# Sharing a PSUM bank between two transposed row blocks, and spreading ten weight loads

## The chip, the cores and the metric

The kernel runs on one core of a Trainium2 chip. The metric is the device time of one execution in microseconds. Five engines matter here: PE (matrix multiplies and transposes), DVE (vector work), ACT (scalar engine, here almost only exponentials), POOL (small vector work and some transfers) and SP, whose queue issues most transfers.

## The reference

Two layers, each an attention block and an MLP, with the same weights in both layers. The input has 2048 rows of 512 in bf16.

```python
x = A_x
x = x + _A_ref(_layernorm(x), A_wqkv, A_wo)   # 32 heads of 16, softmax over 2048 keys
x = x + _B_ref(_layernorm(x), B_w1, B_w2)     # 512 -> 1792, relu, -> 512
x = x + _A_ref(_layernorm(x), A_wqkv, A_wo)
x = x + _B_ref(_layernorm(x), B_w1, B_w2)
return x
```

The layer norm has no scale or shift. For every head 2048 x 2048 exponentials are needed, and that, in two layers, is most of the work outside PE.

## The kernel before

**Tiling.** Rows come in 16 blocks of 128, held as x_t in SBUF, and in chunks of four blocks (512 rows). In the second layer the last two chunks are halved, so that it has six chunks: two of four blocks and four of two. Everything that contracts over the model width needs the normalised rows transposed: ln_transpose transposes one block xnbuf[i] of 128 x 512 on PE in four pieces of 128 x 128 (L535) into a PSUM bank, and a DVE copy (L576) brings the result, 128 x 512 bf16, into xnT, where four such blocks lie side by side for each of the four pieces of the width. ln_groups makes these steps for the n blocks of a chunk.

**Attention.** The main loop goes slot by slot. A slot computes up to three blocks of scores (128 keys x 512 queries; with half chunks, two of 256 for each block) into one of two PSUM tiles ps_s of three banks (L1356). ACT takes the exponential of two or three of them at once (L1365). In some slots the third block goes to DVE instead, which computes the exponential with integer and multiply steps: a first step for each block (L1051), and then a chain over a pair of blocks (L1092, L1103, L1092, L1107, with L1104 in some). PE multiplies the results with the values into ps_o (L944). When a head's segment ends, DVE copies ps_o to u (L858), a transfer c<-u on the SP queue gathers the softmax sums (L863), DVE takes their reciprocal (L885), u<-c brings it back (L886), and the quotient is formed (L874).

**Filler.** All other matrix work (norm transposes, q, k and v, output projection o, the two halves h and z of the MLP) is cut in groups of pieces which PE runs between the scores of the slots. Their matmuls are at L445. In the main loop these groups all use the one bank ps_f, and each ends in one copy out by DVE.

**What sets the order.** The order of instructions on each engine is written by Python at build time: a planner keeps modelled times for PE (now_pe) and DVE (now_dve), a list of what is made and when, and lists of groups (urgent, work) and DVE tasks. A group starts when what it depends on is made (start_group); fill_pe starts no group while an earlier one still waits for its copy (evac), and work is rationed by owed, which grows by a pace in each slot. A piece costs so many units of 216 ns: one transposed block 1.3. The copy of 512 is booked with 342 ns. Between slots run_dve chooses DVE's next instructions, and a pair of blocks is given to DVE when the modelled backlog allows it; in the first layer, after the first pairs, only when the values of all 16 blocks are made. The planner allows the transfer c<-u 3600 ns (C_LAG). If something is needed that is not made, run_until makes it at once. The engines then run their lists in order, whatever the real times.

**Weights of the MLP.** w1 passes through four buffers w1buf of 128 columns each; when an h group is issued, its after() issues the loads that refill the buffers it used (L681). The last half chunk's MLP stands at the end, written out by hand (L1417 and after). For it, w1_last names 14 homes: four are the w1buf, ten are the halves of the tiles kt01 and kt2, free by then. rest_of_chunk issues those ten loads (L766) on the SP queue when the attention of the fourth of the second layer's six chunks ends. A wait of a transfer is made by the queue that issues it, and the queue keeps its order.

Of the kernel before, what the change touches and what calls it, by code (L numbers as in the profile page):

```python
# [12 lines left out]
BF16 = mybir.dt.bfloat16  # L13
# [12 lines left out]
def kernel(  # L26
# [10 lines left out]
    nc = tc.nc  # L37
    P = 128
# [3 lines left out]
    S, D = x_flat.shape  # L42
# [7 lines left out]
    NDC = D // P  # L50
# [50 lines left out]
    def sb(shape, dt, name):  # L101
        return persist.tile(shape, dt, name=name)
# [33 lines left out]
    xnT = [sb([P, NDC, QS], BF16, f"xnT{j}") for j in range(NQS)]  # L136
# [72 lines left out]
    def bank():  # L209
        if ending[0]:  # L210
            bank_no[0] += 1
            return (ps_f[:], ps_s[0][:, 0, :], ps_s[1][:, 0, :])[bank_no[0] % 3]
        if not wide[0]:
            return ps_f[:]
        n = bank_no[0] % 7
        bank_no[0] += 1
        in_bank[0] = (2, 0) if n == 6 else (n // W, n % W)
        if n == 6:
            return ps_f[:]
        return ps_s[n // W][:, n % W, :]  # L220
# [26 lines left out]
    def mark(key, engine="dve", lag=0.0):  # L247
        made[key] = (engine, (now_pe if engine == "pe" else now_dve)[0] + lag)
# [43 lines left out]
    def group(pieces, makes, deps):  # L292
        g = {"pieces": pieces, "makes": makes, "deps": deps}
        maker.update({k: g for k in makes})
        return g

    def put_evac(cost, fn):
        evac.append((cost, now_pe[0] + PE_TO_DVE, fn))
# [85 lines left out]
    def finish_group():  # L384
        while cur:
            do_piece()
        while evac:
            do_evac()
# [24 lines left out]
    def run_all():  # L413
        while True:
            finish_group()
            g = next(
                (g for q in (urgent, work) for g in q if at(g["deps"], "pe") is not None), None
            )
            if g is not None:
                start_group(g)  # L420
            elif dve_q:
                do_task(next(t for t in dve_q if at(t["deps"], "dve") is not None))
            else:
                break
        assert not (urgent or work)
# [104 lines left out]
        )  # L530

    def ln_transpose(tag, i, b=None, at_bank=None):
        pt = (bank() if b is None else b).bitcast(BF16)
        for c in range(NDC):
            ins = nc.tensor.transpose(  # L535
                pt[:, c * P : (c + 1) * P], xnbuf[i][:, c * P : (c + 1) * P], ident[:]
            )
            if wide[0]:
                uses(ins, in_bank[0] if b is None else at_bank)
        mark(("xT", tag, i), "pe")  # L540
        return pt[:, 0 : NDC * P].rearrange("p (c f) -> p c f", c=NDC)
# [24 lines left out]

    def ln_groups(tag, dst, at_column, n, war):
        groups = []
        for i in range(n):

            def piece(i=i):
                pt = ln_transpose(tag, i)

                def fin():
                    a = at_column + i * P
                    nc.vector.tensor_copy(out=dst[:, :, a : a + P], in_=pt)  # L576
                    mark(("xnT", tag, i))

                put_evac(342, fin)

            groups.append(
                group([(1.3, piece)], [("xT", tag, i), ("xnT", tag, i)], [("xn", tag, i)] + war)
            )
        return groups

    def each(n, *key):
        return [key + (i,) for i in range(n)]
# [89 lines left out]
    def load_w1(n):  # L677

        if n < len(chunks) * NF - NF + NW1:
            ft = n % NF  # L680
            nc.sync.dma_start(  # L681
                out=w1buf[n % NW1][:],
                in_=B_w1[:, ft * P : (ft + 1) * P].rearrange("(c p) f -> p c f", p=P),
            )
            mark(("w1", n), "pe", 4000.0)

    def h_group(l, j, ft, war):
        n = (l * NQS + j) * NF + ft
        xj, a, w = columns(l, j)

        number = QS // w
        fts = range(ft, ft + number)
        made_here = [("h", l, j, f) for f in fts]

        def fin(b):
            out = htp[ft // 2][:, ft % 2 : ft % 2 + number, a : a + w]
            sums = b.rearrange("p (f q) -> p f q", f=number)
            if ending[0]:
                nc.scalar.activation(out=out, in_=sums, func=ACTF.Relu)
            else:  # L700
                nc.vector.tensor_scalar(  # L701
                    out=out, in0=sums, scalar1=0.0, scalar2=None, op0=ALU.max
                )
            for key in made_here:
                mark(key)

        def after():
            for f in range(number):
                load_w1(n + f + NW1)

        return mm_group(
            [
                (w1buf[(n + f) % NW1][:, c, :], xnT[xj][:, c, a : a + w])
                for f in range(number) for c in range(NDC)
            ],
            fin, made_here,
            each(w // P, "xnT", ("ln2", l, j)) + war + [("w1", n + f) for f in range(number)],
            after=after, wide_by=w, sums=number,
        )

# [33 lines left out]
    def rest_of_chunk(l, j):  # L754

        if (l, j) == (1, LAST - 2):
            for ft in range(NF):
                home = (
                    w1buf[((l * NQS + LAST) * NF + ft) % NW1] if ft < NW1
                    else (kt01 + kt2)[(ft - NW1) // 2][:, ft % 2, :].rearrange(  # L760
                        "p (c f) -> p c f", c=NDC
                    )
                )
                w1_last.append(home)
                if ft >= NW1:
                    nc.sync.dma_start(  # L766
                        out=home,
                        in_=B_w1[:, ft * P : (ft + 1) * P].rearrange("(c p) f -> p c f", p=P),
                    )
        b = before(l, j)  # L770
        xj, a, w = columns(l, j)
        n = w // P
        war_h = each(chunks[b][1], "z", *b) if b else []
        work[0:0] = [o_group(l, j, i) for i in range(n)] + ln_groups(
            ("ln2", l, j), xnT[xj], a, n, []
        )
        gs = [h_group(l, j, ft, war_h) for ft in range(0, NF, QS // w)]
        gs += [z_group(l, j, i) for i in range((l, j) == (1, LAST - 1), n)]
        if l == 0:
            gs += ln_groups(("ln1", 1, j), xnT[j], 0, TPC, [])  # L780
            gs.append(k_group(1, 0, j))
            gs += [v_group(1, kb) for kb in range(j * TPC, (j + 1) * TPC)]
            gs += [k_group(1, T, j) for T in range(1, 4)]
        return gs
# [342 lines left out]
    tag = ("ln1", 0, 0)  # L1127
    idle_matmuls(24)
    for e in range(2):
        nc.vector.tensor_reduce(  # L1130
            out=mask[e],
            in_=ident[:].rearrange("p (g e d) -> p e g d", g=4, e=2)[:, e],
# [3 lines left out]
            out=qmask[:, e : e + 1], in0=mask[e], scalar1=SCALE * LOG2E * UNIT, scalar2=None,  # L1136
# [8 lines left out]
    for i in range(TPC):  # L1145
        pt = ln_transpose(tag, i)
# [15 lines left out]
    b = plain(k_mms(0, 0))  # L1162
# [6 lines left out]
    b = plain(v_mms(0))  # L1169
# [3 lines left out]
    for j in range(1, NQS):  # L1173
        tag = ("ln1", 0, j)
# [52 lines left out]
    while units:  # L1227
# [6 lines left out]
        for (sg, kb, g), *_ in banked:  # L1234
            if sg["n"] not in seen:
                seen.add(sg["n"])
                n = sg["n"] + 1
# [11 lines left out]
        half = None  # L1249
        if len(banked) == W and pair_at in (None, no):  # L1250
            mine = banked[-1][0][0]
            if pair_at == no:
                half, take = 1, pairs[-1]["sg"]
            elif (not pairs or pair_no[0] + 1 - pairs[0]["n"] < NP) and ((mine['l'] or ("v", 0, 15) in made or not pairs and ("k", 0, 0, 1) in made) and (not mine['l'] or ('k', 1, 0, NQS - 1) in made or pace < PAIR_PACE)):
# [7 lines left out]
                if now_dve[0] + waiting < now_pe[0] + BACKLOG:  # L1262
# [3 lines left out]
                    for n, sg in enumerate(segs[first : here + FAR]):  # L1266
                        till = sum(x is sg or segs.index(x) < segs.index(sg) for x in ahead)
                        if (
# [4 lines left out]
                            half, take = 0, sg  # L1273
# [74 lines left out]
        b = ps_s[no % 2][:].rearrange("p w q -> p (w q)")  # L1348
# [14 lines left out]
        while len(pend) == NE:  # L1363
            force_v()
        ex = nc.scalar.activation(  # L1365
            out=eb[:, 0 : place[m]], in_=b[:, 0 : place[m]], func=ACTF.Exp,
# [27 lines left out]
        run_dve(0.0, musts)  # L1394
    ending[0] = True
    run_all()
    ending[0], wide[0] = False, True
    users.clear()
    l, j = 1, LAST
    tag = ("ln2", l, j)  # L1400
    tt, n_rows = chunks[l, j]
    rows = range(n_rows)
    _, at_column, width = columns(l, j)
    last = slot[0] % 2
    banks = [(1 - last, w) for w in range(W)] + [(2, 0)]
    more = [(last, w) for w in range(W)] + [(3, 0)]
# [4 lines left out]
    def at_bank(b):  # L1411
        n, w = b
        return ps_s[n][:, w, :] if n < 2 else (ps_f, ps_o)[n - 2][:]
# [38 lines left out]

    half_part(0, range(NF))
    for i in rows:
        pt = ln_transpose(tag, i, at_bank(more[i]), more[i])
        copy = nc.vector.tensor_copy if i % 2 else nc.scalar.copy
        uses(copy(out=xnT[NQS - 1][:, :, part(i)], in_=pt), more[i], "xnT")
    for i in rows:
        add(banks[i], ident[:], x_t[tt + i][:], True, False, "x")
    for ft in range(NF + 1):  # L1460
        if ft < NF:
            b = more[ft % 4]
# [5 lines left out]
            if ft % 2:  # L1468
                out = nc.scalar.activation(out=ht[ft][:, at_column : at_column + width], in_=at_bank(b)[:, 0:width], func=ACTF.Relu)
            else:  # L1470
                out = nc.vector.tensor_scalar(
                    out=ht[ft][:, at_column : at_column + width], in0=at_bank(b)[:, 0:width],
                    scalar1=0.0, scalar2=None, op0=ALU.max,
                )
# [7 lines left out]
    for i in rows:  # L1482
# [3 lines left out]
            out=out_flat[(tt + i) * P : (tt + i + 1) * P, :], in_=x_t[tt + i][:]  # L1486
# [31 lines left out]
```

The softmax here doesn't subtract the row's maximum and nothing guards it: scores larger than these inputs give would overflow.

## Time and profile before

The time is 1597.29 us, the median of 3 runs (1595.71 to 1597.43). The profiled execution has a span of 1593.3 us.

| | busy us | share |
|---|---|---|
| ACT | 1553.2 | 97% |
| DVE | 1490.0 | 94% |
| PE | 1437.3 | 90% |
| POOL | 98.4 | 6% |

| rows that the change touches | count | mean ns |
|---|---|---|
| transpose L535, 128 x 128 into ps_f | 232 | 221 |
| copy L576, 128 x 512 bf16 out of ps_f | 58 | 418 |
| load L681, 128 KB, SP queue | 130 | |
| load L766, 128 KB, SP queue | 10 | |

In a group's row the columns are: line, engine, operation, what is written <- what is read, shapes, count | busy us, mean ns of one | idle time of the engine just before, and what ended it. In a timeline row they are: start in us, duration in us, engine, line, operation; a bracket at the end is idle time before it and what ended that. An engine's busy time is the union of its instructions, which can overlap a little, so that the distance from start to start is shorter than the duration of one.

### The profile page before, as it was taken

Reading aid. Unit: us, or ns where it says so; the run is one execution under the profiler, and the core shown is the slowest. Engines: PE = TensorE matmul, PEld = TensorE weight load, DVE = VectorE, ACT = ScalarE, POOL = GpSimd, SP = SyncE. Lnnn points to the kernel's source line nnn. Section 1 sums busy time; section 2 is a strip of 40 time slices with the busy share of each in tenths; the row PEclk is TensorE's granted clock in tenths of the full one; section 3 lists DMA queues with packets and bytes.
Section 4 is the critical chain, followed back from the end, with each engine's and each line's share of the span. In section 5 each row is a group of like instructions: output and inputs, shape, how many; then the busy total and the mean of one; then the engine's idle time right before and its main releaser. Section 6 shows DMA issues by size and latency. Waiting matters only on the chain.

```text
span 1593.3 us, 45167 instructions
## 1 busy us (share of the span) xinstructions
PE 1437.3 (90%) x19793; PEld 539.0 (34%) x19793; DVE 1490.0 (94%) x2899; ACT 1553.2 (97%) x1383; POOL 98.4 (6%) x240
## 2 busy tenths in 40 slices
PE   8888888998999989899888999888999899899897
PEld 3322222222233222233222223222334444445454
DVE  6669999999999999999899999899999999899994
ACT  7999999999999999999999999999999999899994
POOL 2000001001010010100000000001000110010100
PEclk9999999999999999999999999999999999999999
DMA  5001100210012000120000100000211111413020
GB/s 166 1 2 23 20 11 10 46 29 12 5 22 45 19 15 5 29 46 11 14 2 11 31 8 1 2 4 9 55 24 20 36 36 23 93 20 65 14 61 16
DMA packets 115829, 42.42 MB, mean 27 GB/s; under 512 B 104784, under 2 KB 112720, under 8 KB 115632
## 3 DMA queue, kind: packets, MB, share of 16 engines
q1 hardware_dynamic: 101696, 26.21, 7.3%
q0 software_dynamic: 12592, 12.02, 4.2%
q8 instruction: 154, 2.52, 0.6%
q10 hardware_dynamic: 1344, 1.31, 0.2%
q14 instruction: 43, 0.35, 0.1%
HBM read 24.38 MB, written 2.10 MB: 17 GB/s over the span
## 4 chain that ended last, share of the span: by engine, by line
ACT 72%; PE 14%; DVE 11%; issue 2%; SPq 1%; DMA 0%; POOL 0%; ACTq 0%; DVEq 0%
ACT e L1365 72%; PE ps_s L1356 5%; PE ps_f L445 4%; PE ps_o L944 4%; DVE lin L1051 3%; DVE cube L1103 1%; DVE step L1092 1%; DVE cube L1107 1%; PE ps_s L1417 1%; DVE q L643 1%; DVE ht L701 1%; SPq L766 1%; DVE stats L479 0%; DVE u L858 0%; DVE x L727 0%
## 5 line engine op out<-in xcount | busy, mean ns | idle before, releaser
L1365 ACT ACTIVATE e<-ps_s 128x1536 bf16<-128x1536 f32 (+1 forms) x1366 | 1544.6, 1366 | 9.4 <-PE ps_s L1356 8.5
L1356 PE MATMUL ps_s<-q,ktp 32*128 32x512 bf16 (+1 forms) x6121 | 604.6, 340 | 106.2 <-ACT e L1365 96.3
L944 PE MATMUL ps_o<-e,vaug 128*32 128x512 bf16 (+1 forms) x4256 | 496.3, 345 | 12.4 <-DVE u L858 5.4
L1051 DVE TENSOR_SCALAR lin<-ps_s 128x512 int16<-128x512 f32 x684 | 465.5, 685 | 24.1 <-PE ps_s L1356 17.2
L1356 PEld LDWEIGHTS <-ktp 32*128 32x128 bf16 x6121 | 196.3, 91 | 552.2 <-issue 418.0
L944 PEld LDWEIGHTS <-vaug 128*32 128x32 bf16 x6036 | 171.9, 94 | 298.7 <-issue 281.7
L1092 DVE TENSOR_SCALAR step<-lin 128x1024 int16<-128x1024 int16 x684 | 268.8, 419 | 0.6
L1103 DVE TENSOR_TENSOR cube<-step 128x1024 f16<-128x1024 bf16 x342 | 231.8, 681 | 0.6
L1107 DVE TENSOR_TENSOR cube<-cube,lin 128x1024 bf16<-128x1024 f16 x342 | 232.3, 680 | 0.0
L944 PE MATMUL ps_o<-step,vaug 128*32 128x512 bf16 (+1 forms) x864 | 156.0, 339 | 3.2 <-DVE step L1092 3.2
L445 PE MATMUL ps_f<-xnT,w 128*32 128x512 bf16 (+1 forms) x2016 | 151.0, 347 | 6.1 <-DVE ht L701 2.9
L944 PE MATMUL ps_o<-cube,vthird 128*32 128x512 bf16 (+1 forms) x812 | 148.9, 338 | 0.5 <-DVE cube L1107 0.5
L445 PE MATMUL ps_f<-w,ht 128*32 128x512 bf16 x1624 | 146.7, 381 | 1.1 <-DVE q L643 0.8
L944 PE MATMUL ps_o<-lin,vaug 128*32 128x512 bf16 (+1 forms) x864 | 121.7, 338 | 4.8 <-DVE u L858 1.8
L888 POOL DMA_DIRECT2D r<-u x59 | 43.7, 740 | 1176.8 <-DVE lin L1051 383.2
L445 PE MATMUL ps_f<-xnT,wqkv 128*32 128x512 bf16 (+1 forms) x1312 | 106.6, 360 | 5.4 <-DVE ktp L593 0.9
L445 PE MATMUL ps_f<-wo,ot 128*32 128x512 bf16 x960 | 86.3, 381 | 1.1 <-DVE ktp L593 0.8
L701 DVE TENSOR_SCALAR ht<-ps_f 128x512 bf16<-128x512 f32 x105 | 72.0, 686 | 3.3 <-PE ps_f L445 2.1
L445 PEld LDWEIGHTS <-w 128*32 128x32 bf16 x2016 | 60.0, 97 | 37.3 <-issue 21.7
L643 DVE TENSOR_TENSOR q<-ps_f,masks 128x1024 bf16<-128x1024 f32 (+1 forms) x51 | 53.6, 1051 | 12.4 <-PE ps_f L445 7.6
L445 PEld LDWEIGHTS <-ht 128*32 128x32 bf16 x1624 | 45.3, 96 | 28.3 <-issue 12.2
L944 PEld LDWEIGHTS <-vthird 128*32 128x32 bf16 x812 | 44.5, 95 | 30.6 <-issue 27.1
(103 smaller groups left out, 637.7 us busy)
## 6 DMA issues: line engine op xcount, KB each, us to landing
w<-in_B_w_dram SPq DMA_DIRECT2D x130, 128.0 KB
r<-u POOLq DMA_DIRECT2D x32, 256.0 KB, 7.3
r<-u POOLq DMA_DIRECT2D x27, 128.0 KB, 5.0
out_dram<-x SPq DMA_DIRECT2D x16, 128.0 KB
x<-in_A_x_dram SPq DMA_DIRECT2D x14, 128.0 KB
w<-in_B_w_dram SPq DMA_DIRECT2D x1, 1792.0 KB
ktp<-in_B_w_dram SPq DMA_DIRECT2D x10, 128.0 KB
wqkv<-in_A_wqkv_dram ACTq DMA_DIRECT2D x2, 512.0 KB
```

Of the source, the lines that this page charges most:

```text
L445: nc.tensor.matmul(out[cols], lhsT[:, cols], rhs, start=i % k == 0, stop=i % k == k - 1, tile_position=(0, 32 * g), skip_group_check=True,)
L643: return nc.vector.tensor_mul(out=qbuf[n % 2][:, :, 0:w], in0=b.rearrange("p (e q) -> p e q", e=1).to_broadcast((P, 2, w)), in1=qmask.rear ...
L701: nc.vector.tensor_scalar(out=out, in0=sums, scalar1=0.0, scalar2=None, op0=ALU.max)
L766: nc.sync.dma_start(out=home, in_=B_w1[:, ft * P : (ft + 1) * P].rearrange("(c p) f -> p c f", p=P),)
L888: nc.gpsimd.dma_start(out=r[:, 0:width], in_=bass.AP(tensor=sums.tensor, offset=sums.offset, ap=[list(sums.ap[0]), [0, 32], [1, width]],),)
L944: nc.tensor.matmul(ps_o[32 * g : 32 * g + 32, 0 : sg["w"]], values[:, 4 * sg["T"] + g, 2 * e : 2 * e + 32], rhs, start=g not in sg["begun" ...
L1051: first = nc.vector.tensor_scalar(out=lin[which][:, half * QS : (half + 1) * QS], in0=src, scalar1=EXP_BIAS, scalar2=0.0, op0=ALU.add, op1 ...
L1092: nc.vector.tensor_scalar(out=stair, in0=line, scalar1=keep, scalar2=put, op0=ALU.bitwise_and, op1=ALU.bitwise_or,)
L1103: (609, lambda: nc.vector.tensor_mul(out=power, in0=mantissa, in1=mantissa)),
L1107: (609, lambda: nc.vector.tensor_mul(out=power.bitcast(BF16), in0=power, in1=line.bitcast(BF16))),
L1356: nc.tensor.matmul(b[:, a : a + sg["w"]], kt[32 * g : 32 * g + 32, kc : kc + P], qbuf[sg["n"] % 2][32 * g : 32 * g + 32, sg["e"], 0 : sg[" ...
L1365: ex = nc.scalar.activation(out=eb[:, 0 : place[m]], in_=b[:, 0 : place[m]], func=ACTF.Exp, scale=1.0 / (LOG2E * UNIT),)
```

## The change

Two edits. First, in ln_groups two row blocks share a group: each is transposed into its half of one bank (512 bf16 of the 1024 that fit), and one copy of 128 x 1024, booked with 609 ns, brings both into xnT. This halves the number of copies, of bank turns and of groups. A group now depends on both blocks. The transposes of the first and of the last chunk, which stand outside the main loop, still go one by one. Second, the ten loads for the last MLP are put in a list when they become due, and each later h group issues one, after its own loads, so that they don't fill the SP queue all at once.

```diff
-        for i in range(n):
-
-            def piece(i=i):
-                pt = ln_transpose(tag, i)
+        for i in range(0, n, 2):
+            hold = {}
+
+            def piece(k):
+                if not k % 2:
+                    hold["b"] = bank()
+                half = hold["b"].bitcast(BF16)[:, k % 2 * D : (k % 2 + 1) * D]
+                ln_transpose(tag, k, half)
+                if not k % 2:
+                    return
+                pt = hold["b"].bitcast(BF16).rearrange("p (i c f) -> p c i f", i=2, c=NDC)
 
                 def fin():
-                    a = at_column + i * P
-                    nc.vector.tensor_copy(out=dst[:, :, a : a + P], in_=pt)
-                    mark(("xnT", tag, i))
-
-                put_evac(342, fin)
+                    a = at_column + (k - 1) * P
+                    nc.vector.tensor_copy(
+                        out=dst[:, :, a : a + 2 * P].rearrange("p c (i f) -> p c i f", i=2), in_=pt
+                    )
+                    for of in (k - 1, k):
+                        mark(("xnT", tag, of))
+
+                put_evac(609, fin)
 
             groups.append(
-                group([(1.3, piece)], [("xT", tag, i), ("xnT", tag, i)], [("xn", tag, i)] + war)
+                group(
+                    [(1.3, lambda k=k, piece=piece: piece(k)) for k in (i, i + 1)],
+                    [("xT", tag, k) for k in (i, i + 1)] + [("xnT", tag, k) for k in (i, i + 1)],
+                    [("xn", tag, k) for k in (i, i + 1)] + war,
+                )
             )
...
+    w1_to_load = deque()
...
         def after():
             for f in range(number):
                 load_w1(n + f + NW1)
+            if w1_to_load:
+                home, of = w1_to_load.popleft()
+                nc.sync.dma_start(
+                    out=home,
+                    in_=B_w1[:, of * P : (of + 1) * P].rearrange("(c p) f -> p c f", p=P),
+                )
...
                 if ft >= NW1:
-                    nc.sync.dma_start(
-                        out=home,
-                        in_=B_w1[:, ft * P : (ft + 1) * P].rearrange("(c p) f -> p c f", p=P),
-                    )
+                    w1_to_load.append((home, ft))
```

More of the change, by code (lines that the diff above doesn't have):

```diff
@@ L532, in ln_transpose @@
     def ln_transpose(tag, i, b=None, at_bank=None):
-        pt = (bank() if b is None else b).bitcast(BF16)
+        pt = bank().bitcast(BF16) if b is None else b
         for c in range(NDC):
@@ L1396 @@
     run_all()
+    assert not w1_to_load
     ending[0], wide[0] = False, True
@@ L1454 @@
     for i in rows:
-        pt = ln_transpose(tag, i, at_bank(more[i]), more[i])
+        pt = ln_transpose(tag, i, at_bank(more[i]).bitcast(BF16), more[i])
         copy = nc.vector.tensor_copy if i % 2 else nc.scalar.copy
```

## The prediction

> **What bounds the kernel now.** I read the page first, then the groups with shapes kept apart, then the windows, then the timelines of the one window that stood out.
>
> ```profile
> PE 1437.3 (90%) x19793; PEld 539.0 (34%) x19793; DVE 1490.0 (94%) x2899; ACT 1553.2 (97%) x1383; POOL 98.4 (6%) x240
> ACT 72%; PE 14%; DVE 11%; issue 2%; SPq 1%; DMA 0%; POOL 0%; ACTq 0%; DVEq 0%
> ```
>
> ACT sets the end: it is idle for only 1593.3 - 1553.2 = 40.1 us. The windows say where: 11.5 us before 20 us (the prologue), 21.3 us after 1550 us (the last MLP by hand), and of the 7.2 us between them 4.92 us lie in one window, 1360 to 1400. All other seams together leave 2.3 us. So a change can gain in three ways: fewer exponentials on ACT, a shorter prologue or tail, or that one gap. The page also lists SPq L766, the burst of ten weight loads, at 1% of the chain: a queue that should never be on it.
>
> The groups show what ACT's work consists of and how DVE shares it (columns: count | busy us, mean ns of one | idle before):
>
> ```profile
> L1365 ACT ACTIVATE e<-ps_s 128x1536 bf16<-128x1536 f32 x681 | 1024.1, 1576 | 8.2 <-PE ps_s L1356 7.6 <-PE ps_o L944 0.5
> L1365 ACT ACTIVATE e<-ps_s 128x1024 bf16<-128x1024 f32 x684 | 739.3, 1157 | 1.2 <-PE ps_s L1356 0.9
> L576 DVE COPY xnT<-ps_f 128x512 bf16<-128x512 bf16 x58 | 24.2, 418 | 3.1 <-PE ps_f L535 2.8
> L535 PE MATMUL ps_f<-ident,xn 128*128 128x128 bf16 x232 | 22.9, 221 | 2.6 <-DVE xnT L576 0.8 <-DVE xn L526 0.6 <-DVE q L643 0.5
> ```
>
> Half of the slots hand one block of 512 columns to DVE; that makes the exponential 1576 - 1157 = 419 ns shorter, so a pair of blocks on DVE is worth 0.84 us of ACT. Lines L576 and L535 are all that the first edit touches: 58 copies, 232 transposes.
>
> The window 1360 to 1400, in slices (PE, PEld, DVE, ACT, POOL busy, clock, DMA share, GB/s), and DVE there:
>
> ```profile
> 1375.00:1380.00 5.00, 3.88 (x89) 2.21 (x88) 1.83 (x4) 5.00 (x5) 0.00 (x0) 1.00 0.67 140
> 1380.00:1385.00 5.00, 2.67 (x43) 1.66 (x46) 3.98 (x10) 0.79 (x2) 0.00 (x0) 0.57 0.52 114
> 1385.00:1390.00 5.00, 5.00 (x98) 2.80 (x90) 3.85 (x7) 4.29 (x5) 0.00 (x0) 0.75 0.24 52
> ```
> ```profile
> 1372.76 0.41 DVE L858 COPY u<-ps_o 128x256 f32<-128x256 f32 x1
> ...
> 1376.15 0.68 DVE L1107 TENSOR_TENSOR cube<-cube,lin 128x1024 bf16<-128x1024 f16 x1
> 1380.58 0.20 DVE L885 RECIPROCAL c<-c 128x8 f32<-128x8 f32 x1 [3.75 <-DMA c<-u]
> ```
>
> The sync queue and ACT in the same window:
>
> ```profile
> 1369.87 8.57 SPq L766 DMA_DIRECT2D ktp<-in_B_w_dram  x10
> 1378.54 0.56 SPq L863 DMA_DIRECT2D c<-u  x1
> ```
> ```profile
> 1384.60 1.45 ACT L1365 ACTIVATE e<-ps_s 128x1536 bf16<-128x1536 f32 x1 [4.21 <-PE ps_s L1356]
> 1386.76 14.66 ACT L1365 ACTIVATE e<-ps_s 128x1024 bf16<-128x1024 f32 x13 [0.71 <-PE ps_s L1356]
> ```
>
> Read them as one story. DVE has the softmax sums copied at 1372.76 + 0.41 = 1373.17. Their small transfer c<-u could be issued then, but the sync queue is busy with ten loads until 1378.44. It goes out at 1378.54 and takes 2.02 us (chain of waits); DVE waits 3.75 us for it with all its later work behind, PE waits 3.17 us for DVE (its L944 row at 1382.33), and ACT runs dry for 4.21 us and again for 0.71 us, the second while PE's clock is down at 0.57 to 0.75. Nowhere else does DVE wait longer than 3.8 us for c<-u: the waits list gives it 4.0 us in two waits, this one and a trifle.
>
> **What the skill says.** (1) "DMA: Bandwidth & Descriptors", Anatomy of one DMA: a semaphore wait happens on the issuing sequencer before dispatch, and a transfer has a fixed cost of some 2.0 us. So whatever stands ahead of c<-u on the queue delays it; the trace agrees, with the queue busy for 8.57 us and 2.02 us for c<-u. (2) "VectorE: DVE Perf Modes", Why PSUM operands drop a tier and the table of the errata section: a bf16 copy out of PSUM runs at most two per cycle, 120 + FD/2 cycles at 0.96 GHz: 392 ns for 512 and, an estimate from that page, 658 ns for 1024. The trace has 418 ns for 512, so two per cycle it is. (3) "PSUM — Partial Sum Buffer", The four PSUM rules: a bank is 2 KiB per partition; two blocks of 512 bf16 fill it exactly, so the second block fits. No run here shows that yet. (4) "TensorE: Matmul & The Clock Gate", What's actually happening: a mostly idle PE has its clock lowered. The 0.57 after the 3.17 us wait agrees.
>
> **Part 1, the weight loads.** Removed: the burst. Its ten loads go out one after each h group, behind the one or two loads of w1 that the group issues anyway. L701 rows stand at 1374.95, 1381.26 and 1385.79, so h groups are running when the loads become due, and fourteen more (seven for each of two half chunks) follow before the last MLP needs them. Cost: the same ten issues of about 0.51 us (their median), now spread; the sync queue has room, and no compute engine waits on the loads until 1570 us. A c<-u that comes just after a group finds at most one more load ahead. Gain: in the window above c<-u would go out at about 1373.2 and land at 1373.2 + 0.05 + 2.02 = 1375.3, before DVE turns to the reciprocal at 1376.83. DVE's 3.75 us wait goes, and with it ACT's 4.21 + 0.71 = 4.92 us. Even with one slow load of 2.33 us ahead it lands at 1377.6, a wait of 0.8 us. Bounds: 3.0 us (3.75 less 0.8) to 4.9 us; I take 4.9, since on the free queue nothing else fills the time.
>
> **Part 2, the shared bank.** PE: the same 232 transposes, no change. DVE: 58 copies become 29 of 1024. From start to start the neighbours of such rows show 0.33 us for a 418 ns instruction (L1092 at 1371.82, next at 1372.15) and 0.60 us for a 680 ns one (L1107 at 1370.62, next at 1371.22). I put the 1024 copy in the latter class: twice the 267 ns of streaming plus the same 151 ns is 685 ns. So 58 x 0.33 = 19.1 us becomes 29 x 0.60 = 17.4 us, 1.7 us saved; by the full durations, 24.2 - 29 x 0.685 = 4.3 us. The other end, if the new order of the output (two blocks swapped with four) lost the two per cycle, is the fp32-like row L643 of 1024 at 1220 ns: 29 x 1.14 = 33 us, 14 us lost. I take the first: innermost runs stay 128 elements on both sides, as in the 418 ns copy. DVE's saving counts only as exponentials taken from ACT: a pair costs DVE (465.5 + 268.8 + 231.8 + 232.3 + 10.3) / 342 = 3.53 us and frees 0.84 us, so 1.7 us is worth 0.4 us (4.3 us: 1.0 us).
>
> Moved: the filler groups share one bank, ps_f, and the planner starts no group while one waits to be copied out, so a transpose group takes a slot of about 1.1 us for 0.40 us of PE. Copies in the first stage stand at 38.20, 39.25 and 40.59. Six slots fewer before the last v group (113.0 us) would bring the point at which DVE may take pairs freely, about 115 us, up to 6 x 1.1 = 6.6 us forward. Before that DVE takes 11 first steps in 95 us; afterwards 9 in 15 us. 6.6 x (0.60 - 0.12) = 3.2 blocks of 0.42 us is 1.3 us at most; half-used, as the v groups are held by PE's spare time and not by the bank, 0.6 us. Added waits: a group starts only when both its row blocks are normalised, so the first waits one L526 more (0.33 us), and the bank is held until the second is transposed (0.40 us on PE). Both delay only filler, which has slots of slack while ACT is fed; I cost them at nothing.
>
> **Sum.** 4.9 + 0.4 + 0.6 = 5.9 us; I take 0.2 off for a load that may still stand ahead of a c<-u and use 5.7. 1597.3 - 5.7 = 1591.6 us.
>
> **Rivals.**
> *A new stall takes the old one's place (17%).* The order is written by a planner with estimated costs, so from the first shared bank at 37 us on every group lands elsewhere, and DVE has no slack (94%) to hide a late transfer. One such event costs about what this one did: 5.7 - 4.9 leaves 0.8 us, 1596.5 us. Against: of 78 such transfers before, one did this, and it had a burst ahead of it.
> *Slower by the new order (14%).* Two such stalls, or one and five pairs fewer on DVE (5 x 0.84): 1591.6 + 9.8 = about 1601 us. For: 99% of DVE is booked in most windows; the run before leaves only 2.3 us in seams, little to gain and more to lose. Against: the pairs are gated by queued work, which shrinks.
> *The wide copy falls to one per cycle (4%).* 14 us more DVE: as 4 pairs lost, 3.3 us; as stalls, since the planner books 609 ns, the full 14: 1595 to 1606, centre 1600.
> *More comes of it (10%).* The longer DVE saving (1.0), the whole 1.3 us, and fewer blocked slots in the later filler stages, two or three pairs more: 1591.6 - 3.5 = 1588 us.
>
> **Chances and range.** The forecast, within 2.5 us of 1591.6, has 55%. Faster than 1594.1 (0.2%): nearly all of that and the 10%, 0.66. Within 0.2%: the replaced stall, 0.17. Slower: 0.17. The range reaches from 1587.5, just under the best case, to 1600, which takes in one stall and part of the slower cases.
>
> **What will show it.** L766 gone as a burst; no DVE wait on c<-u above 1 us; ACT's gap list between 20 and 1550 us under 4 us in all; PE's clock at 1.00 there. The copy x29 at about 685 ns (1200 would be the third rival). The first steps L1051 at 684 or a few more; 676 or fewer means the planner gave pairs up. The last v copy of layer 0 at 107 to 112 us. The prediction is wrong if ACT waits for scores appear in the seams at 100 to 130, 550 to 600, 700 to 780 or 1140 to 1180 us.

## The result, and the profile after

The changed kernel takes 1592.40 us, the median of six runs (1591.72 to 1594.34), against 1598.02 us for the kernel before in the same session: a ratio of 0.9968 (here and below not the quotient of the two medians), with a 95% interval of 0.9955 to 0.9980, or 5.1 us with an interval of 3 to 7 us. The forecast was 1591.6 us.

First the page of the changed kernel, with the engines' busy time and the shares of the chain:

```profile
PE 1431.9 (90%) x19801; PEld 538.6 (34%) x19801; DVE 1490.7 (94%) x2876; ACT 1552.1 (98%) x1383; POOL 100.1 (6%) x240
ACT 80%; PE 8%; DVE 8%; issue 2%; DMA 1%; POOL 0%; SPq 0%; ACTq 0%; DVEq 0%
```

ACT's busy time fell by only 1.1 us, yet the chain runs through ACT for 80% of the span and no longer for 72%: what went is time in which ACT had nothing to do. The groups say where the 1.1 us comes from (count | busy us, mean ns of one | idle before):

```profile
L1384 ACT ACTIVATE e<-ps_s 128x1536 bf16<-128x1536 f32 x679 | 1021.1, 1576 | 4.5 <-PE ps_s L1375 3.7 <-PE ps_o L963 0.3
L1384 ACT ACTIVATE e<-ps_s 128x1024 bf16<-128x1024 f32 x686 | 740.8, 1156 | 0.6 <-PE ps_s L1375 0.6
L583 DVE COPY xnT<-ps_f 128x1024 bf16<-128x1024 bf16 x29 | 19.8, 682 | 2.8 <-PE ps_f L535 2.7
L535 PE MATMUL ps_f<-ident,xn 128*128 128x128 bf16 x232 | 20.1, 222 | 2.0 <-DVE xnT L583 1.8
```

Two slots more hand a block to DVE (686 for 684): one pair, 0.84 us of the 1.1; most of the rest is one single exponential of 128x512 that took 597 ns and not 850. The wide copy takes 682 ns, near the forecast 685 and far from the 1220 ns of the slow case (L643 of 1024), so it kept the rate of the narrow copy.

Next the sync queue where the burst used to be:

```profile
1368.31 5.15 SPq L695 DMA_DIRECT2D w<-in_B_w_dram  x4
1373.50 0.50 SPq L728 DMA_DIRECT2D ktp<-in_B_w_dram  x1
1374.10 0.57 SPq L882 DMA_DIRECT2D c<-u  x1
1377.51 1.47 SPq L695 DMA_DIRECT2D w<-in_B_w_dram  x2
1379.02 0.50 SPq L728 DMA_DIRECT2D ktp<-in_B_w_dram  x1
```

One of the ten loads stands ahead of c<-u in place of all ten, behind the four of w1, and c<-u goes out at 1374.10, right when the sums are copied (L877 at 1373.66 + 0.41 us). The windows there (PE, PEld, DVE, ACT, POOL busy, clock, DMA share, GB/s), DVE's reciprocal and ACT:

```profile
1375.00:1380.00 5.00, 4.91 (x134) 2.77 (x126) 5.00 (x12) 5.00 (x7) 0.00 (x0) 1.00 0.28 62
1380.00:1385.00 5.00, 4.64 (x124) 2.82 (x112) 4.74 (x12) 5.00 (x6) 0.00 (x0) 1.00 0.60 135
1385.00:1390.00 5.00, 4.36 (x97) 2.22 (x95) 5.00 (x12) 5.00 (x6) 0.00 (x0) 1.00 0.36 79
```
```profile
1379.86 0.19 DVE L904 RECIPROCAL c<-c 128x8 f32<-128x8 f32 x1
```
```profile
1358.80 42.21 ACT L1384 ACTIVATE e<-ps_s 128x1536 bf16<-128x1536 f32 x38
```

No bracket follows the reciprocal, and ACT runs 42 us without one: no wait, no gap, the clock at 1.00. Between 20 and 1550 us ACT is now idle for 1530 - 1527.25 = 2.75 us; before it was 7.2 us. In the four seams that the prediction named as signs of being wrong, ACT's idle time is 0.28 us in all, and was 1.96 us. Of the 4.5 us so gained and the 1.1 us of busy time, 2.2 us are lost again at the end of this profiled run, where PE's clock fell (0.73 and 0.58) while the last values were summed (ACT's wait for PE that follows is 6.2 us, and 4.2 us before):

```profile
1555.00:1560.00 5.00, 4.20 (x67) 2.26 (x61) 3.98 (x9) 4.79 (x4) 0.00 (x0) 0.73 0.00 0
1560.00:1565.00 5.00, 5.00 (x41) 2.41 (x39) 2.19 (x5) 1.03 (x2) 0.00 (x0) 0.58 0.01 3
```

So the spans of the two profiled runs differ by only 3.4 us. Such drops come and go from run to run; a fit over all runs of this study gives about 0.9 us more for each 0.001 of mean granted clock less. Below, "at equal clock" means the time brought to a clock of 0.995 by that fit: before 1597.3, the changed kernel 1593.3 us (within 0.6). This is a rough measure, and it hides a part of the burst's price: the stall itself took the clock to 0.57 and 0.75 in two windows of 5 us, by which the mean over the span falls by some 0.002 (5 x 0.43 + 5 x 0.25 = 3.4 us of 1593). By the fit that is about 2 us, an estimate, which "at equal clock" leaves out of the burst's price. For each kernel the plain median and its ratio to the kernel before on the same chip come first.

### The profile page after: what moved, and what is told of

Read it like the earlier page. It is cut to its first block, busy times and chain, and to the rows that moved or that the text cites. A ratio compares the mean times of both kernels' runs of the same rounds, so it can differ in the third digit from the quotient of the medians.

```text
span 1589.9 us, 45152 instructions
## 1 busy us (share of the span) xinstructions
PE 1431.9 (90%) x19801; PEld 538.6 (34%) x19801; DVE 1490.7 (94%) x2876; ACT 1552.1 (98%) x1383; POOL 100.1 (6%) x240
## 4 chain that ended last, share of the span: by engine, by line
ACT 80%; PE 8%; DVE 8%; issue 2%; DMA 1%; POOL 0%; SPq 0%; ACTq 0%; DVEq 0%
ACT e L1384 80%; PE ps_s L1375 3%; DVE lin L1070 2%; PE ps_f L445 2%; PE ps_o L963 2%; DVE step L1111 1%; PE ps_s L1437 1%; DVE cube L1126 1%; DVE cube L1122 1%; DVE ht L717 1%; DMA r<-u 0%; DMA wqkv<-in_A_wqkv_dram 0%; DVE q L657 0%; DVE ot L893 0%; DVE stats L479 0%
## 5 line engine op out<-in xcount | busy, mean ns | idle before, releaser
L1384 ACT ACTIVATE e<-ps_s 128x1024 bf16<-128x1024 f32 (+1 forms) x1366 | 1543.4, 1365 | 5.1 <-PE ps_s L1375 4.3
L445 PE MATMUL ps_f<-xnT,w 128*32 128x512 bf16 (+1 forms) x2016 | 146.7, 345 | 5.5 <-DVE ht L717 2.8
L963 PE MATMUL ps_o<-step,vaug 128*32 128x512 bf16 (+1 forms) x868 | 151.0, 340 | 0.0
L963 PE MATMUL ps_o<-cube,vthird 128*32 128x512 bf16 (+1 forms) x816 | 144.1, 338 | 0.0
L445 PE MATMUL ps_f<-wo,ot 128*32 128x512 bf16 x960 | 91.7, 381 | 1.0 <-DVE x L681 0.9
```

Of the source, the lines that this page charges most:

```text
L445: nc.tensor.matmul(out[cols], lhsT[:, cols], rhs, start=i % k == 0, stop=i % k == k - 1, tile_position=(0, 32 * g), skip_group_check=True,)
L963: nc.tensor.matmul(ps_o[32 * g : 32 * g + 32, 0 : sg["w"]], values[:, 4 * sg["T"] + g, 2 * e : 2 * e + 32], rhs, start=g not in sg["begun" ...
L1384: ex = nc.scalar.activation(out=eb[:, 0 : place[m]], in_=b[:, 0 : place[m]], func=ACTF.Exp, scale=1.0 / (LOG2E * UNIT),)
```

## The experiments

**The two edits apart.** The planner doesn't book the loads, so the second edit alone leaves PE, DVE and ACT in the order of before, and the first alone gives them that of the changed kernel. In the traces DVE and ACT keep these two orders, instruction for instruction.

```diff
 # e1_loads: before, with the second edit only
+                    w1_to_load.append((home, ft))
 # e2_bank: after, with the burst kept
-                    w1_to_load.append((home, ft))
+                    nc.sync.dma_start(out=home, in_=B_w1[...])
```

> Only the second edit: ten loads spread, transposes and copies as before. The planner does not book loads, so PE, DVE and ACT get the order of before. Theory (queue order): the 3.75 us wait of the reciprocal and ACT's 4.9 us gap go, and nothing else changes: 3.0 to 4.9 us faster than before, about 1593.5 us. Rival (the gain of the change comes from the new order that the shared bank brings): within 1 us of before, about 1597.5 us.

> Only the first edit: shared bank and wide copy, but the ten loads issued at once as before; engines have the order of the changed kernel. Theory: one pair more on DVE and seams as in the changed kernel, 1 us faster than before by itself, but the burst meets whatever c<-u stands near it; in the changed kernel a c<-u stands at 1374, close after the last loads of h groups, so the burst delays it by up to 6 us and a stall of 0 to 5 us remains: 1593 to 1598 us. Rival (the stall was an accident of the old order): no stall in the new order, the same time as the changed kernel, 1592.4 us.

Loads alone: 1592.05 us against 1597.64, ratio 0.9966 (0.9955 to 0.9977). Bank alone: 1594.28 us, ratio 0.9980 (0.9972 to 0.9988). At equal clock 1593.4 and 1594.9, with 1593.3 for both edits together. The loads alone bring all of the gain, so the first theory holds. Their trace has c<-u on the queue as soon as the sums are copied (1373.65 + 0.42 us), no wait at the reciprocal, and no gap of ACT:

```profile
1374.10 0.56 SPq L868 DMA_DIRECT2D c<-u  x1
```
```profile
1338.93 81.77 ACT L1370 ACTIVATE e<-ps_s 128x1536 bf16<-128x1536 f32 x73
```

Between 20 and 1550 us ACT is idle for 2.6 us there, 4.6 us less than before. That the bank alone brings more than half has its reason mostly in the order: the burst still stands ahead of c<-u, which goes out at 1380.03, but in the new order DVE comes to the reciprocal 5.9 us after copying the sums, and not 3.7 us, so less of the delay shows. DVE and ACT with the bank alone:

```profile
1382.05 0.20 DVE L907 RECIPROCAL c<-c 128x8 f32<-128x8 f32 x1 [1.79 <-DMA c<-u]
```
```profile
1384.77 5.54 ACT L1387 ACTIVATE e<-ps_s 128x1024 bf16<-128x1024 f32 x5 [2.93 <-PE ps_s L1378]
```

1.79 us in place of 3.75, and 2.93 in place of 4.92. The gains of the two edits are not to be added: they are two ways of losing less at one place.

**Fewer loads at once.**

```diff
+                if NW1 <= ft < NW1 + 5:
+                    nc.sync.dma_start(out=home, in_=B_w1[...])
+                elif ft >= NW1:
+                    w1_to_load.append((home, ft))
```

> The kernel before with five of the ten loads at once and five one by one. Theory (queue order): in the trace of before the fifth load is out at about 1372.3 us, before the sums are copied at 1373.2, so c<-u goes out at once, and there is no wait: the time of all ten spread, about 1593.5 us. Rival (any burst on the transfer engines delays c<-u, in proportion): half of the wait stays, about 1.9 us, and 1595.5 us.

1594.06 us, ratio 0.9974 (0.9964 to 0.9985); at equal clock 1593.6, the time of ten spread. In its trace the five take the queue for 3.25 us, to 1377.08, the sums are copied at 1377.14, and c<-u goes out at 1377.17. DVE doesn't wait for it, its wait for the way back u<-c is 0.52 us, and ACT has no gap. What counted for c<-u was that the queue was free when it was wanted; the five loads then under way cost almost nothing.

**The burst on another queue.**

```diff
-                    nc.sync.dma_start(
+                    nc.gpsimd.dma_start(
```

> The kernel before with the burst of ten loads kept in one place, but issued on POOL's queue, so that it moves the same bytes at the same time and doesn't stand ahead of c<-u. Theory (order on the SP queue): the wait of the reciprocal is under 1 us and the time is that of spread loads, about 1593.5 us. Rival (the ten loads fill the transfer engines, and c<-u would be late on any queue): the wait stays at 2 to 4 us and the time within 2 us of before.

1596.78 us, ratio 0.9994 (0.9982 to 1.0006), so no gain by the plain times; at equal clock 1596.1, 1.2 us better than before and 2.7 us short of spread loads. Neither theory alone is right. The wait for c<-u is gone, but new ones are there. POOL's queue, DVE, PE and ACT:

```profile
1378.11 7.83 POOL L766 DMA_DIRECT2D ktp<-in_B_w_dram  x10
```
```profile
1382.56 0.19 DVE L885 RECIPROCAL c<-c 128x8 f32<-128x8 f32 x1
1389.06 0.01 DVE L898 LOAD_MASK_SELECT r<-u  x1 [2.56 <-DMA u<-c]
```
```profile
1386.11 0.73 PE L445 MATMUL ps_f<-xnT,w 128*32 128x256 bf16 x20 [1.09 <-DMA w<-in_B_w_dram]
1387.21 3.28 ACT L1365 ACTIVATE e<-ps_s 128x1536 bf16<-128x1536 f32 x3 [1.20 <-PE ps_s L1356]
```

The way back, u<-c, was issued at 1383.77 on a free sync queue and yet DVE had to wait for it until 1389.06. PE waited too, for a w1 load from the sync queue, and ACT's gap of 1.20 us comes right after that wait, ahead of DVE's. So the burst has a second price, which the order of one queue doesn't explain: while the ten loads were being sent, this small transfer took 5.25 us, where c<-u took 2.02 us in the kernel before. That this is the filling of the transfer engines is a reading; no run took it apart.

**The same burst, one place further back, and a planner that knows of the delay.** In the first of these the ten loads go out at once just behind the c<-u; the engines' order is that of before. In the second the burst stays where it was, and the planner allows this one c<-u 9600 ns; from there on it draws a new order, with one pair more for DVE.

```diff
 # e12_behind, after the issue of c<-u
+                while w1_to_load:
+                    home, of = w1_to_load.popleft()
+                    nc.sync.dma_start(out=home, in_=B_w1[...])
 # e8_lag
-                mark(("c", n), lag=C_LAG)
+                mark(("c", n), lag=C_LAG + (6000.0 if late else 0.0))
```

> The kernel before with its burst of ten loads whole, but issued just behind the one c<-u transfer that it stood ahead of; PE, DVE and ACT keep their order of before. If the late c<-u is all that the burst cost: ACT has no gap near 1375 us and the time is that of spread loads, 1592 to 1594 us. If whatever stands behind the burst pays, the loads of w1 for the next h groups too: PE waits 1 to 4 us for a w1 load, and 1594.5 to 1597.5 us. I take the second, 1595.5 us, after the run with the longer allowance, in which PE waited for such a load.

> The kernel before with its burst of ten loads on the SP queue, but the planner is told that the one c<-u transfer behind the burst takes 9600 ns in place of 3600, so that DVE is given other work first and comes to the reciprocal later. The transfer is as late as before. Theory (what costs is DVE standing at a reciprocal that comes too early in its order, with all else queued behind): the 3.75 us wait shrinks to under 1 us and 3 to 4.5 us are gained, about 1594 us. Rival (the late sums themselves hold up what needs them, the output projection and its followers): no gain, about 1597.5 us.

Behind: 1600.23 us, ratio 1.0018 (1.0007 to 1.0029), even slower than before. Longer allowance: 1599.36 us, ratio 1.0008 (1.0000 to 1.0016), no gain. In both the wait for c<-u is gone. With the burst behind it, PE, DVE and ACT show this instead:

```profile
1385.98 1.26 PE L445 MATMUL ps_f<-xnT,w 128*32 128x256 bf16 x20 [5.12 <-DMA w<-in_B_w_dram]
```
```profile
1387.70 0.01 DVE L902 LOAD_MASK_SELECT r<-u  x1 [5.44 <-DMA u<-c]
```
```profile
1387.83 1.45 ACT L1369 ACTIVATE e<-ps_s 128x1536 bf16<-128x1536 f32 x1 [5.86 <-PE ps_s L1360]
```

The w1 loads for the next h group stand behind the ten, start at 1382.79, and PE is kept from its filler, and so from the scores behind it, for 5.12 us. With the longer allowance the chain of waits goes the same way: a w1 load from 1384.56 for 2.41 us, then PE, and ACT is idle for 2.31 us. That is less than the 4.92 us of before, and yet nothing is gained; since the order is new from here on, the first of the two runs is the cleaner one. The theory that only the reciprocal's place in DVE's order costs has fallen: in each of these runs something else behind the burst paid, and taking one transfer out of the way handed the bill to the next.

**What a microsecond of DVE costs that nobody booked.** Each wide copy is made twice.

```diff
+                    nc.vector.tensor_copy(
+                        out=dst[:, :, a : a + 2 * P].rearrange("p c (i f) -> p c i f", i=2), in_=pt
+                    )
```

> The changed kernel with each of the 29 wide copies made twice, which the planner does not know of: 29 x 0.60 = 17.4 us more on DVE, everything else in the same order. It prices an unbooked DVE microsecond, and so what the forecast's third rival (a wide copy at one element per cycle, 14 us more) would have cost. If DVE time comes out in full: 17 us slower than the changed kernel, about 1610 us. If slack in the order swallows it: under 5 us slower, 1592 to 1597 us. I take 7 us, about 1600 us, since DVE is booked at 99% but its work waits in buffers ahead of PE.

1612.55 us, ratio 1.0086 (1.0072 to 1.0100). DVE is busy for 1507.8 - 1490.7 = 17.1 us more, and at equal clock the time grows by 14.7 us. My guess of 7 us was half of it; nearly the full DVE time comes out.

**How far two orders of the same work lie apart.** Only the number that the planner books for the copy is changed. On the chip the work is nearly the same: with the order the planner also moves a pair or two of blocks between ACT and DVE (first steps on DVE: 684 with the loads alone, 686 in e10_book and e6_book; 686 with both edits, 690 in e7_book, 684 in e9_book) and repeats some matmuls more.

```diff
 # with the loads alone: e6_book, e10_book
-                put_evac(342, fin)
+                put_evac(350, fin)   # e10_book: 338
 # the changed kernel: e7_book, e9_book
-                put_evac(609, fin)
+                put_evac(620, fin)   # e9_book: 600
```

> Loads spread, transposes and copies of one block as before, but the copy booked with 350 ns in place of 342: no work is added, only the planner's order changes. Theory (a new order by itself moves the time little as long as no burst lies in it): within 2.5 us of the kernel with the loads alone, 1590.5 to 1595 us. Rival (a new order is a lottery of several us): more than 3 us away from it.

> The changed kernel with the wide copy booked with 620 ns in place of 609: again only the order changes. Together with the run before it shows how far two orders of the same work lie apart, and so whether the shared bank's own share of the gain can be told from zero. Theory: within 2.5 us of the changed kernel, 1590 to 1595 us. Rival: more than 3 us away.

> The changed kernel with the wide copy booked with 600 ns in place of 609: only the planner's order changes, a second draw of an order for the shared bank beside the one with 620 ns (1592.3 us). If orders of this kernel mostly come out alike: 1590 to 1595 us. If the 21 us that 8 ns of booking cost the kernel with the loads alone is the usual scatter: more than 5 us from 1592.4 us. I think the first has 60%.

> Loads spread, transposes and copies as before, the copy booked with 338 ns in place of 342; a second draw beside the one with 350 ns (1613.4 us), which stood 10.7 us at a reciprocal's round trip that its planner had been forced into. If such forced steps are rare: 1591 to 1596 us. If they are usual in this kernel: over 1597 us. I think the first has 55%.

| kernel | booked ns | us | ratio to before | at equal clock |
|---|---|---|---|---|
| loads alone | 342 | 1592.05 | 0.9966 (0.9955 to 0.9977) | 1593.4 |
| e10_book | 338 | 1595.30 | 0.9991 (0.9978 to 1.0004) | 1595.9 |
| e6_book | 350 | 1613.43 | 1.0097 (1.0084 to 1.0110) | 1609.6 |
| both edits | 609 | 1592.40 | 0.9968 (0.9955 to 0.9980) | 1593.3 |
| e7_book | 620 | 1592.30 | 0.9960 (0.9947 to 0.9973) | 1593.6 |
| e9_book | 600 | 1598.83 | 1.0003 (0.9990 to 1.0016) | 1596.6 |

Of the four draws one equals the order that it starts from (0.3 us apart at equal clock), two are 2.5 and 3.3 us slower and one is 16 us slower. That one has a new stall, at another seam. DVE and POOL's queue in e6_book:

```profile
1183.09 0.25 DVE L890 RECIPROCAL c<-c 128x16 f32<-128x16 f32 x1
1194.04 0.75 DVE L879 SCALAR_TENSOR_TENSOR ot<-u,masks,r 128x512 bf16<-128x512 f32 x1 [10.70 <-DMA r<-u]
```
```profile
1186.73 0.69 POOL L893 DMA_DIRECT2D r<-u  x1 [40.64 <-issue]
```

In DVE's order the product follows the reciprocal at once, though two transfers lie between (1.82 and 7.29 us in the chain of waits). That is what run_until does when a segment ends and its buffer u is still in use; that it was called here follows from the order, it was not recorded. DVE stands for 10.70 us, PE for 9.09, ACT for 9.28 and once more for 4.26 us. e9_book has no stall of that kind. In its profiled run ACT is idle for 10.5 us between 20 and 1550 us, and 7.0 us of that lie in five windows of 10 us with a low clock, such as these:

```profile
840.00:850.00 10.00, 8.88 (x60) 1.90 (x59) 8.38 (x16) 9.17 (x9) 3.49 (x9) 0.65 0.01 2
850.00:860.00 10.00, 10.00 (x70) 2.50 (x67) 7.20 (x15) 7.44 (x7) 0.00 (x0) 0.50 0.00 1
```

The clock isn't the whole of it, since at equal clock e9_book is still 3.3 us slower than the changed kernel; one pair fewer on DVE is worth 0.84 us of that, and the rest stays open.

**A try for a faster version: more work on PE against clock drops.**

```diff
-    FLOOR = 0.56
+    FLOOR = 0.60
```

> The changed kernel with PE's least load raised from 0.56 to 0.60 of a slot, so that it repeats more score matmuls and has fewer drops of its granted clock. Over all runs so far a clock lower by 0.001 goes with 0.8 us more. Theory (the drops cost the time): the mean clock rises from 0.9957 to 0.998 or more and the time falls by about 2 us, to 1590.5 us, if the new order is as good. Rival (the repeated matmuls, or the new order, cost more): slower than 1593.5 us.

1597.48 us, ratio 1.0001 (0.9988 to 1.0014). The mean clock was 0.9946, no higher than the changed kernel's 0.9957, with 230 more matmuls. The theory fell: more repeated matmuls in a new order did not keep the clock up, and at equal clock this order is 4.6 us slower. No run beat the changed kernel beyond doubt; the loads alone and e7_book equal it.

## Why the prediction was right

*Part 1, the loads: right in mechanism and size.* The step said 3.0 to 4.9 us, with 4.9 taken. The loads alone measured 0.34% (0.23 to 0.45), 5.4 us by the ratio and 3.9 us at equal clock (which takes the stall's own clock drop out). The steps inside held as well: the engines' order is unchanged, c<-u goes out when the sums are there, DVE's 3.75 us and ACT's 4.92 us are gone. What was incomplete is the list of who pays. The prediction followed only the reciprocal; the burst kept behind c<-u showed that w1 loads and the way back u<-c pay as much (5.12 and 5.44 us of waiting). It made no difference here because the edit spreads the loads and doesn't only move them.

*Part 2, the shared bank: each term near its size, the sum not seen.* The copy: 685 ns forecast, 682 measured. DVE's saving becoming exponentials taken from ACT: one pair more, worth 0.84 us of ACT, against 0.4 + 0.6 us. The last v copy of the first layer: forecast 107 to 112 us, measured 110.86 us (113.02 before), 2.2 us earlier where I had used half of 6.6. But the loads alone are as fast as both edits within 0.8 us at equal clock, so the 1.0 us that I added for this part can't be shown in the time. Orders of nearly the same work lay 0.3 to 16 us apart, so a gain of 1 us can't be read off.

*The unknown costs at nothing*, the later start and the longer hold of the bank: show on PE only: its idle time ahead of the transposes, waiting for the copy before, went from 0.8 to 1.8 us in all (while all of its idle time there fell from 2.6 to 2.0), and no gap of ACT over 0.15 us comes within 2 us after one of these waits. An order drawn anew would hide a small cost of this kind.

*The rivals.* "A new stall takes the old one's place" and "slower by the new order" did not come. I gave them 31% together, and they were nearer than that: of four further orders two were about 3 us and one 16 us slower at equal clock. The size of the second was too small as well: I had put it at 1601 us, and an 8 ns change of a booking, in the kernel with the loads alone, gave 1613 us, which lies outside my range. So the time came out as forecast for the reason given, with a share of luck in the order that the shared bank drew. The third rival, a copy at one element per cycle, would have cost nearly its upper end: 17.1 us of unbooked DVE gave 14.7 us, so 14 us would give about 12, an estimate.

*The sum.* Measured are 5.1 us by the ratio, against 5.7. The total fits; that the first term alone accounts for it, within what the times can tell, is what the experiments add.

## What to carry to other kernels

The sync queue kept its order here (c<-u, ready at 1373.17 us, went out at 1378.54, behind the ten), so look at what stands behind a group of transfers issued together: here ten loads that nobody needed for some 200 us cost about 5 us, because a small transfer with an engine waiting on it stood behind them. Moving the group by one place, to another queue, or telling the planner of one victim left most or all of the cost here, with another victim; spreading the transfers over the queue's gaps removed it.

When a kernel's order comes out of a planner, compare edits in the same order of the engines wherever that can be had (the loads were not booked, so it could), and draw a few orders before crediting an edit of one or two microseconds.

A DVE microsecond saved and one lost need not be worth the same in such a kernel: saved and booked, it can buy 0.84 us of ACT for 3.53 us of DVE, the price of a pair in the prediction; lost and not booked, it came out at 14.7 us for 17.1.

## What the runs showed of the hardware

Ten loads of 128 KB in rows of 256 bytes took the sync queue 8.57 us in the kernel before: most issues 0.51 us, two of them 2.33 and 1.57 us. POOL's queue took 7.83 us for the same ten.

PE's granted clock fell to 0.50 in a window of 10 us in which PE counts as busy throughout (e9_book, 850 to 860 us). But the drop began near 843 us, after PE had been busy for only 1.49 and 1.44 us of the two windows of 2 us from 838 to 842, with no gap over 0.62 us, and at half the clock the same work fills the time. This is the usual picture: the 14 traces, cut into windows of 2 us from 20 to 1540 us, have 36 places where the clock falls below 0.98 after two windows at full clock. Before 30 of them PE was busy for less than 80% of the last 4 us, which holds for only 11% of all stretches of 4 us at full clock. Most of these light stretches (some 1065 of 1095) bring no drop, and a higher floor of PE work did not raise the mean clock (0.9946 against 0.9957). What decides which light stretch brings a drop stays open.
